# Turning two more normalized slices by DMA instead of the tensor engine, with a new instruction order (two-layer long-convolution and MLP kernel)

## The chip, the core and the metric

The kernel runs on one core of a Trainium2 chip. A core has five engines that run their own instruction streams side by side: TensorE (PE, matrix multiplication and transposes, results in PSUM), VectorE (DVE), ScalarE (ACT), GpSimd (POOL) and SyncE (SP, which here issues nearly all DMAs). They meet through semaphores. The metric is the time of one execution on the device in microseconds (us), lower is better.

## The reference

Four residual steps are applied to a sequence of 2048 rows of 512 channels, in bfloat16: A, B, A, B. Step A is a gated long convolution, step B is an MLP with a GELU.

```
def _A_ref(q, k, v, shift_k, ssm_k, ssm_D):
    ...
    kv = k_shift * v
    ...
    y = y + kv * ssm_D[None, None, :]
    return q * y

def _B_ref(x, w1, b1, w2, b2):
    y = _layernorm(x, axis=-1)
    h = _gelu(jnp.einsum("bsd,df->bsf", y, w1) + b1)
    return jnp.einsum("bsf,fd->bsd", h, w2) + b2

x = A_q
x = x + _A_ref(_layernorm(x, axis=-1), A_k, A_v, A_shift_k, A_ssm_k, A_ssm_D)
x = x + _B_ref(_layernorm(x, axis=-1), B_w1, B_b1, B_w2, B_b2)
x = x + _A_ref(_layernorm(x, axis=-1), A_k, A_v, A_shift_k, A_ssm_k, A_ssm_D)
x = x + _B_ref(_layernorm(x, axis=-1), B_w1, B_b1, B_w2, B_b2)
return x
```

The convolution y depends only on k, v and the filters, not on x. So the kernel computes it once, in a front part, and both A steps use it. After that each row of x goes through the four steps on its own.

## The kernel before

**Front part.** The convolution is a transform over the sequence, done as two stages of small matrix products, a product with the transformed filter, and two inverse stages. The stages that later text names are: the short filter on k and its product with v (lines 800 to 850, for two channel groups on TensorE with L832 behind it, for two on VectorE at L656), the first transform stage (L764), the second stage of the filter (L777) and of the data (L870), the products with the filter (L656 with 128x2048 tiles), the first inverse stage (L894, 256 matmuls) and the second inverse stage (L951, 64 matmuls). The channels are cut into two parts of 64 groups of four (`PARTS`), and products and inverse stages run part by part. Every stage leaves its result in PSUM, and an evacuation copies it to SBUF: L661 when ScalarE does it, L662 when VectorE does. Either engine can take one.

**Row part.** The 2048 rows are 16 slices of 128 rows; slice s is `R_X + s * 512`. Two layers (`L` is 0 and 1) of one A and one B step follow. A layer goes through its slices in blocks: 1, 1, 2, 2, 2, 2, 2, 2, 2 slices in layer 0 and four blocks of 4 in layer 1. For a block, with tags q, y, z, m1 and m2:

- q: mean and variance of each slice on VectorE (L983, L985), the inverse root on POOL (L989, L991), normalization on VectorE (L998)
- y: product with y and residual addition (L656 with 128x512 tiles; 128x256 for the first four slices)
- z: the same statistics and normalization again, into a rotating set of eight buffers
- turning: the first MLP product contracts over channels, so the normalized slice z must be turned, channels into partitions. For slices 0 to 3 of layer 0, TensorE does four 128x128 transposes into PSUM (L1045), and ScalarE or VectorE copies the result to the buffer `R_XT` (L661 or L662). For all other slices, SP issues one `dma_start_transpose` from z to `R_XT` (L1037). There are two `R_XT` buffers, taken by turns of the blocks
- m1: 11 chunks of 4 matmuls (L1058), each followed by ScalarE's GELU (L1063) into `R_HT`
- m2: 11 matmuls per slice (L1091) with a residual addition on VectorE (L1095); the last slice is cut into pieces (L1080, L1084). Finished slices of layer 1 go out by DMA (L645).

**Order.** Nothing in the program text fixes the order of the instructions on an engine. Each piece of work is recorded with `P.op`, with what it reads and writes and with a duration in nanoseconds. `Prog.schedule` then runs a planner: engine by engine it takes the piece that can start first by these durations, and among equals the one of highest priority. It also chooses between ScalarE and VectorE for each evacuation. A DMA takes, in the planner, its issue time and then its bytes at 370 per ns and 2300 ns. Large hand-over tables, keyed by tag or by the running number of the piece, bend the plan: `BIAS` and `PB` are added to priorities, `HOLD` gives an earliest start, `PS` and `SHY` handicap VectorE for an evacuation, and `ENG` forces an evacuation to one engine. On the chip only the resulting order counts, with semaphore waits that `Prog.sync` puts in. SP's queue is in order too: a DMA that waits for its source holds the ones behind it.

Of the kernel before, what the change touches and what calls it, by code (L numbers as in the profile page):

```python
# [44 lines left out]
class Prog:  # L45
# [6 lines left out]
    BIAS = {'': -521155, 'fir0': 1051798, 'fir1': 843097, 'fir2': 989049, 'fir3': 987651, 'h1': 1081037, 'h2': -15927, 'ht': 1112634, 'i1_0': 1897872, 'i1_64':  # L52
        1957624, 'i2_0': 1184460, 'i2_64': 1481308, 'm1': 2555275, 'm2': -1895730, 'q0': 888240, 'q1': 774644, 'q19': 368770, 'q2': 596884, 'q20':
        169092, 'q21': -27345, 'q22': 917115, 'q3': 746810, 'q4': 810080, 'q5': 973212, 'q6': 1402410, 'q7': 321282, 'q8': 747916, 'taps': 871203,
        'warm0': 1001221367, 'x1_0': 904949, 'x1_1': 332081, 'x1_2': 669567, 'x1_3': 179302, 'x2_0': 377722, 'x2_64': 1746588, 'y0': 402006, 'y1':
        377011, 'y19': 351016, 'y2': 526293, 'y20': 1353266, 'y21': 1084298, 'y22': 962110, 'y3': 501697, 'y4': 829124, 'y5': 1453849, 'y6': 1171227,
        'y7': 417695, 'y8': 201523, 'z0': 1335006, 'z1': 1302874, 'z19': 54792, 'z2': 645169, 'z20': 1225188, 'z21': 742421, 'z22': -322863, 'z3':
        -681085, 'z4': 290073, 'z5': -723046, 'z6': 31881, 'z7': 125204, 'z8': 150269}
    SHY = {'fir0': 1381, 'fir1': 0, 'h1': 616, 'h2': 0, 'ht': 1476, 'i1_0': 1122, 'i1_64': 0, 'i2_0': 355, 'i2_64': 600, 'x1_0': 0, 'x1_1': 0, 'x1_2': 0,
        'x1_3': 0, 'x2_0': 175, 'x2_64': 0, 'z0': 1278, 'z1': 0, 'z2': 218}  # L60
    PB = {0: 34576, 2: -79378, 3: 43127, 4: 998812279, 9: 1394230, 44: 1395437, 45: 1613596, 47: 734111, 49: 928776, 51: 998512784, 52: 998468674, 53: -251398,
        54: -275617, 55: -73100, 56: -94401, 57: -104470, 58: -97344, 59: -11254, 60: -108406, 61: -94351, 63: -1000973, 64: -999971, 65: 27771, 66:
        -77522, 67: -999603, 68: 141227, 69: -1000923, 70: -1052691, 71: 34934, 72: -77472, 73: 998216537, 74: 133836, 75: -847532, 76: -193783, 77:
        998086816, 78: 213997, 79: -845232, 80: -158480, 81: 998714645, 82: -29228, 83: 998096074, 85: -912875, 86: 81387, 87: -823698, 88: -168262,
        89: 998118247, 90: 94211, 91: 998328931, 92: 27535, 93: -765996, 94: -165174, 95: -789736, 96: -295, 97: -846123, 99: -845182, 100: -158430,
        101: 998114703, 102: -218608, 103: 998118297, 104: -163885, 105: 998086766, 106: 912895, 107: -54439, 108: 950031, 109: -33246, 110: 1149468,
        111: -31803, 112: 1348311, 113: 217100, 114: 974687, 115: 999587069, 116: 918924, 117: 999198541, 118: 903029, 119: 999587119, 120: 909361,
        121: 217391, 122: 694743, 123: 999618935, 124: 958333, 125: 999612320, 126: 1042905, 127: 219847, 128: 900863, 129: 999657213, 130: 964412,
        131: 999608609, 132: 768388, 133: 999620187, 134: 856071, 135: 999410698, 136: 724031, 137: 999546617, 155: 23799, 156: -162015, 157: -60642,
        158: -461494, 159: -153347, 161: -694106, 162: 1454, 163: -947997, 164: 207759, 165: 998395730, 166: -173754, 167: 998555574, 169: 998332526,  # L70
        170: -423295, 171: 998606664, 172: 38904, 173: 998455595, 175: 999072054, 176: 243913, 177: 154045, 178: 391385, 179: 999289091, 180: 348447,
        181: 999128447, 183: 29584, 184: -999103, 185: 998165866, 186: 998199123, 187: 998019345, 188: 998017691, 189: 998151553, 191: -646236, 192:
        -539651, 193: 998734714, 194: -523620, 195: 998581986, 196: -137633, 197: 998715658, 199: 86734, 200: 998494190, 201: 21973, 202: -495859,
        203: 47162, 204: 48952, 205: 59976, 207: 999452991, 208: -1197, 209: 878201, 210: 929976, 211: 999077641, 212: 730704, 213: 999240348, 215:
        999293389, 216: 725624, 217: 510366, 218: 999271422, 219: 646616, 220: 381726, 221: 999070258, 222: 94055, 223: 349589, 224: 999293339, 225:
        71120, 226: -10853, 227: 772848, 228: 711543, 229: 2558, 230: 999128706, 231: 107444, 232: -203830, 233: 1276613, 234: 384777, 235: -85060,
        236: 790445, 237: 75982, 239: -823960, 240: -697909, 241: 997632090, 242: -339336, 243: -1075953, 244: -656610, 245: -826734, 246: 50, 247:
        -1076003, 248: -339386, 249: 997632040, 250: -210520, 251: -489040, 252: -675432, 253: -825900, 255: -927034, 256: -854615, 257: -1353528,
        258: 997762488, 259: -607871, 260: -1334318, 261: -871126, 262: 997876284, 263: -1321, 264: -704597, 265: 997906582, 266: 148883, 267:
        -675809, 268: -909457, 269: -70780, 270: -56569, 271: -864218, 272: -104560, 273: -36737, 274: -577323, 275: -1480713, 276: -833598, 277:  # L80
        997878740, 279: -1162936, 280: 27, 281: -687297, 282: -121406, 283: -1363624, 284: -118911, 285: 997939634, 286: 577508, 287: -393821, 288:
        475975, 289: -885280, 290: -270112, 291: 997939684, 292: 576726, 293: 998145513, 308: 1177488, 309: 1198831, 310: 1304423, 311: 1244639, 312:
        971190, 314: 285666, 315: -57020, 316: 391644, 317: -46141, 318: 998762253, 319: -155518, 320: 135422, 321: -64658, 322: 346129, 324:
        998409091, 325: -1207668, 326: 998414402, 327: -319349, 328: -1037091, 329: -441577, 330: -1032463, 331: -1024485, 332: -884533, 334: -54361,
        335: -51188, 336: -3436, 337: 322745, 339: -19921, 340: 770364, 341: 119508, 343: 150496, 344: -815052, 345: -1074024, 346: -1087676, 347:
        -942418, 348: -900262, 349: -695458, 350: 351759, 351: -892088, 352: 1076614, 353: -2671, 354: 885814, 355: -1190402, 356: 1001895, 357:
        -1433063, 358: 1027075, 359: -1429074, 360: 1029921, 361: -1731382, 362: 919746, 363: -910238, 364: 41149, 365: -890772, 366: 1184682, 367:
        -897821, 368: -1245948, 369: -144705, 370: -1245720, 371: -401600, 372: 2730439, 373: 4887400, 374: 3740474, 375: 2124032, 377: 112340, 378:
        10032, 379: -338853, 380: -245578, 382: 104508, 383: 805647, 384: -77071, 386: -911065, 387: -70724, 388: -451068, 389: -405580, 390: -950972,
        391: -206569, 392: 187780, 393: 885471, 394: -1662575, 395: 1009734, 396: -1295021, 397: 1024703, 398: -1183431, 399: 1037432, 400: -1248538,  # L90
        401: -255605, 402: -654317, 403: -359159, 405: -1278286, 407: 1092663, 408: -888363, 409: 917474, 410: 814, 411: 890156, 412: -211373, 413:
        -358377, 414: 32750, 415: 5020518, 416: 4338250, 417: 3211311, 418: 2415420, 420: -46159, 421: -2327, 422: -267214, 423: 164122, 424: 265989,
        425: -113051, 427: 110610, 428: 892080, 429: 111401, 430: -44629, 431: -261436, 432: -173254, 433: -363932, 434: 23598, 436: 42311, 437:
        12952, 438: -285134, 439: -300486, 440: 216702, 441: 228190, 442: 255444, 443: 205358, 444: 625548, 445: -22042, 446: 108479, 447: 664113,
        448: 1243693, 449: 863420, 450: -179909, 451: -322256, 452: -471129, 453: 1004937, 454: -629654, 455: 863470, 456: -761928, 457: 1009668, 458:
        -890636, 459: -156707, 460: -292462, 461: -1267645, 462: -913360, 463: -782357, 464: -540612, 465: -252368, 466: -913588, 467: -1302020, 468:
        -435191, 469: -251282, 470: -907822, 471: 3209413, 472: 3720996, 473: 4860599, 474: 3269555, 475: 3378084, 476: 4978144, 477: 4979058, 478:
        2905911, 480: -367979, 481: -368512, 482: -100350, 483: -498935, 484: 138365, 485: -92505, 487: -76592, 488: -174921, 489: 24557, 490: 185584,
# [478 lines left out]
def bass_interleave_layers__ssm_conv_h3__mixer_channel_mlp__prompt_kernel(  # L577
# [348 lines left out]
    for p0, n, o, c in ((0, 128, 0, 10), (0, 96, 10, 1)):  # L926
        d, s = M(p0, n, M_B1 + o, [1, c]), A(p0, n, R_B1 + o, [1, c])
# [204 lines left out]
```

## Time and profile before

| What | us |
|---|---|
| median of 4 runs | 243.22 |
| lowest and highest run | 241.5, 244.19 |
| the profiled execution, its own time | 243.8 |
| its span, first to last instruction | 242.0 |
| POOL busy in it | 34.0 |
| TensorE weight loads, beside the matmuls | 154.0 |
| granted TensorE clock, mean over the span | 1.000 |

The profiled execution took 1.8 us more than its span, and 0.58 us more than the median. In the profile a matmul's row shows start and duration of a pipelined instruction, so the durations of a run of matmuls overlap; from start to start, one of L1091 (512 columns) takes about 0.216 us and one of L1058 with 256 columns about 0.108 us. "x4" behind a row is a count of instructions, and a bracket such as "[0.45 <-POOL sm L991]" says how long the engine was idle just before and what ended it. Instruction names keep their order on one engine, but from one engine to another they have to be matched by time.

### The profile page before, as it was taken

The page shows a single profiled execution, that of the slowest core. Times are in us where ns is not written, and L with a number is a line of the kernel's source. Part 1 is how long each engine was busy: PE and PEld are TensorE (multiplying, and loading weights), DVE is VectorE, ACT ScalarE, POOL GpSimd, SP SyncE. Part 2 cuts the span into 40 slices and gives each one's busy share as a digit, 9 for nine tenths or more (in the row PEclk, how much of TensorE's full clock was granted, in tenths as well). Part 3 has the DMA queues.
Part 4 walks back from the last instruction along what each step waited for, and adds up shares of the span by engine and source line. Part 5 has one row for each costly group of instructions (what it writes and reads, how often), then busy time and mean ns, then how long its engine had stood idle before and what let it go on. Part 6 is the DMA issues. An engine that isn't in the chain of part 4 may idle for free.

```text
span 242.0 us, 5585 instructions
## 1 busy us (share of the span) xinstructions
PE 230.5 (95%) x2338; PEld 154.0 (64%) x2338; DVE 179.4 (74%) x366; ACT 140.1 (58%) x222; POOL 34.0 (14%) x75
## 2 busy tenths in 40 slices
PE   5999999976899999999999999999999999999996
PEld 1887777775889887675775684654444444444444
DVE  0489999999999999889999999999977300202223
ACT  2189999989995996544572471446412774124400
POOL 3250000000104121331232104030111000000000
DMA  6999979999990000211221102407041100411003
GB/s 230 340 384 385 385 163 206 191 195 237 397 362 27 3 0 3 43 23 27 43 43 24 22 1 46 81 7 88 1 87 43 46 0 0 87 43 46 35 30 108
DMA packets 35947, 27.14 MB, mean 112 GB/s; under 512 B 18418, under 2 KB 28881, under 8 KB 35922
## 3 DMA queue, kind: packets, MB, share of 16 engines
q1 hardware_dynamic: 35358, 26.65, 41.4%
q8 instruction: 18, 0.29, 0.5%
q10 hardware_dynamic: 564, 0.14, 0.4%
q14 instruction: 7, 0.06, 0.1%
HBM read 16.82 MB, written 2.10 MB: 78 GB/s over the span
## 4 chain that ended last, share of the span: by engine, by line
PE 57%; DVE 24%; ACT 6%; issue 6%; POOL 4%; DMA 2%; DVEq 0%; POOLq 0%
PE ps L1091 26%; PE ps L1058 26%; DVE ar L656 13%; ACT ar L661 6%; DVE sm L983 4%; DVE ar L662 3%; PE ps L894 3%; POOL ar L739 2%; DMA ar<-ar 2%; DVE ar L832 1%; DVE ar L998 1%; PE ps L1080 1%; DVE sm L985 1%; POOL sm L991 1%; PE ps L870 1%
## 5 line engine op out<-in xcount | busy, mean ns | idle before, releaser
L1063 ACT ACTIVATE ar<-ps,sm 128x256 bf16<-128x256 f32 (+4 forms) x143 | 68.3, 522 | 75.0 <-PE ps L1058 71.3
L1058 PE MATMUL ps<-ar 128*128 128x256 bf16 (+4 forms) x572 | 83.1, 297 | 0.1
L1091 PE MATMUL ps<-ar 128*128 128x512 bf16 (+1 forms) x341 | 79.9, 379 | 0.0
L661 ACT ACTIVATE ar<-ps 128x1024 bf16<-128x1024 f32 (+2 forms) x78 | 70.8, 1026 | 12.5 <-PE ps L764 5.6
L1058 PEld LDWEIGHTS ps<-ar 128*128 128x128 bf16 (+1 forms) x572 | 53.3, 100 | 29.1 <-DMA ar<-ar 0.6
L656 DVE TENSOR_TENSOR ar<-ar 128x512 bf16<-128x512 bf16 (+3 forms) x108 | 64.4, 628 | 1.2 <-ACT ar L661 0.4
L1091 PEld LDWEIGHTS ps<-ar 128*128 128x128 bf16 (+1 forms) x341 | 33.1, 98 | 35.1 <-ACT ar L1063 0.4
L1095 DVE TENSOR_TENSOR ar<-ar,ps 128x512 bf16<-128x512 bf16 x31 | 20.8, 677 | 43.7 <-PE ps L1091 43.6
L983 DVE BATCH_NORM_STATS2 sm<-ar 128x6 f32<-128x512 bf16 (+1 forms) x68 | 42.7, 650 | 0.3
L998 DVE TENSOR_SCALAR ar<-ar,sm 128x512 bf16<-128x512 bf16 x64 | 23.5, 403 | 3.6 <-POOL sm L991 3.6
L991 POOL TENSOR_TENSOR sm<-sm 128x2 f32<-128x2 f32 (+2 forms) x26 | 20.2, 777 | 2.2
L764 PE MATMUL ps<-ar 128*64 128x128 bf16 x512 | 18.0, 222 | 1.4 <-ACT ar L661 0.6
L662 DVE CAST ar<-ps 128x1024 bf16<-128x1024 f32 x16 | 18.9, 1208 | 0.0
L989 POOL TENSOR_SCALAR sm<-sm 128x2 f32<-128x2 f32 (+2 forms) x26 | 5.4, 207 | 91.5 <-DVE sm L985 91.3
L764 PEld LDWEIGHTS ps<-ar 128*64 128x64 bf16 x512 | 15.2, 111 | 4.0 <-ACT ar L661 1.8
L894 PE MATMUL ps<-ar 128*128 128x128 bf16 x256 | 14.8, 219 | 0.9 <-DVE ar L656 0.9
L894 PEld LDWEIGHTS ps<-ar 128*128 128x128 bf16 x256 | 14.4, 113 | 1.2 <-DVE ar L656 1.2
L662 DVE COPY ar<-ps 128x2048 bf16<-128x2048 bf16 (+1 forms) x8 | 7.4, 919 | 10.0 <-PE ps L747 10.0
L870 PE MATMUL ps<-ar 128*128 128x64 bf16 x256 | 9.6, 193 | 3.3 <-ACT ar L661 1.9
L985 DVE BATCH_NORM_AGGREGATE sm<-sm 128x2 f32<-128x6 f32 (+1 forms) x64 | 11.1, 177 | 0.7
L870 PEld LDWEIGHTS ps<-ar 128*128 128x128 bf16 x256 | 8.2, 98 | 4.7 <-ACT ar L661 3.0
L777 PE MATMUL ps<-ar 128*128 128x128 bf16 x128 | 8.7, 220 | 0.5 <-ACT ar L661 0.2
(33 smaller groups left out, 78.0 us busy)
## 6 DMA issues: line engine op xcount, KB each, us to landing
ar<-tab_s SPq DMA_DIRECT2D x16, 256.0 KB, 10.0
ar<-ar SPq DMA_DIRECT2D x16, 256.0 KB, 6.1
ar<-in_A_ssm_k_dram SPq DMA_DIRECT2D x4, 512.0 KB, 6.0
ar<-in_A_k_dram SPq DMA_DIRECT2D x8, 256.0 KB, 7.8
ar<-in_A_v_dram SPq DMA_DIRECT2D x8, 256.0 KB, 9.8
ar<-in_A_q_dram SPq DMA_DIRECT2D x4, 512.0 KB, 8.3
out_dram<-ar SPq DMA_DIRECT2D x7, 256.0 KB, 2.0
ar<-in_B_w_dram SPq DMA_DIRECT2D x1, 1376.0 KB, 12.2
```

The lines of the kernel that those rows point to most:

```text
L656: return P.op(eng, lambda e: e.tensor_tensor(o, a, b, op), dur, reads=[a, b] + list(more), writes=[o])
L661: return e.activation(dst, src(), AF.Copy)
L662: return e.tensor_copy(dst, src())
L764: r = e.matmul(Q(tl, 64 * ri, 64, i * 128, [1, 128]), w, m, start=True, stop=True)
L894: r = e.matmul(Q(tl, 0, 128, i * 128, [1, 128]), w, m, start=q == 0, stop=q == 1)
L983: P.op(DVE, lambda e, sj=sj, x=x: e.bn_stats(sj, x), 40.0 + 1.1 * w, reads=[x], writes=[sj], gate=gate)
L991: P.op(POOL, lambda e: e.tensor_tensor(r, v, hf, ALU.pow), 430.0 + 150.0 * n, reads=[v, hf], writes=[r])
L998: P.op(DVE, lambda e: e.tensor_scalar(o, x, m, r, ALU.subtract, ALU.mult), 335.0, reads=[x, m, r], writes=[o])
L1058: r = e.matmul(Q(tl, 0, rows, 0, [1, w]), a, m, start=dk == 0, stop=dk == 3)
L1063: P.op(ACT, lambda e, dst=dst, tl=tl, rows=rows, bias=bias, w=w: e.activation(dst, Q(tl, 0, rows, 0, [1, w]), AF.Gelu_apprx_tanh, bias=bia ...
L1091: r = e.matmul(Q(tl, 0, 128, 0, [1, 512]), ins[fc][0], ins[fc][1], start=fc == 0, stop=fc == 10)
L1095: P.op(DVE, lambda e, x=x, tl=tl: e.tensor_tensor(x, x, Q(tl, 0, 128, 0, [1, 512]), ALU.add), 640.0, reads=[x], writes=[x], tile=tl)
```

## The change

One condition is changed. In layer 0, slices 2 and 3 now take the branch that slices from 4 on took before: one `dma_start_transpose` each, in place of four TensorE transposes and one evacuation. Slices 0 and 1 keep the tensor engine. Two pieces of work fewer are recorded, so every later running number shifts, and all six tables of the planner are replaced by others; no entry of `PB` or `HOLD` keeps its value. `ENG` forces 46 evacuations in place of 63. Durations, blocks, buffers and the planner itself stay as they are.

```
-    BIAS = {'': -521155, 'fir0': 1051798, 'fir1': 843097, 'fir2': 989049, 'fir3': 987651, 'h1': 1081037, 'h2': -15927, 'ht': 1112634, 'i1_0': 1897872, 'i1_64':
...
-    SHY = {'fir0': 1381, 'fir1': 0, 'h1': 616, 'h2': 0, 'ht': 1476, 'i1_0': 1122, 'i1_64': 0, 'i2_0': 355, 'i2_64': 600, 'x1_0': 0, 'x1_1': 0, 'x1_2': 0,
-        'x1_3': 0, 'x2_0': 175, 'x2_64': 0, 'z0': 1278, 'z1': 0, 'z2': 218}
...
+    SHY = {'fir0': 187, 'fir1': 1275, 'h1': 149, 'h2': 0, 'ht': 1293, 'i1_0': 240, 'i1_64': 0, 'i2_0': 872, 'i2_64': 661, 'x1_0': 794, 'x1_1': 0, 'x1_2': 551,
+        'x1_3': 32, 'x2_0': 0, 'x2_64': 0, 'z0': 1489, 'z1': 1251}
...
+    PS = {83: 479, 87: 603, 89: 792, 95: 971, 99: 0, 101: 0, 107: 63, 163: 1004, 165: 0, 167: 1448, 245: 13, 247: 615, 249: 524, 324: 0, 332: 477}
...
@@ -1032,7 +1029,7 @@
                 z = ntmp()
                 norm(s, mr[i], A(0, 128, z, [1, 512]))
                 dst = A(0, 128, R_XT + k * 2048 + i * 128, [512, 4], [1, 128])
-                if L or s >= 4:
+                if L or s >= 2:
                     zs = A(0, 128, z, [1, 512])
                     P.op(SP, lambda e, zs=zs, dst=dst: e.dma_start_transpose(dst, zs), 1300.0, reads=[zs], writes=[dst],
                          dma=True, nbytes=1 << 17)
```

## The prediction

> **What bounds the kernel now.** I read the page's busy times first, then busy time by stretches, then the rows of the turned slices on each engine, and the chain of waits last. The stretches are cut where the chain changes its engine. Columns: stretch, its length, busy us and count of PE, weight loads, DVE, ACT and POOL, granted clock, DMA share, GB/s.
>
> ```profile
> PE 230.5 (95%) x2338; PEld 154.0 (64%) x2338; DVE 179.4 (74%) x366; ACT 140.1 (58%) x222; POOL 34.0 (14%) x75
> ```
>
> ```profile
> 16.50:71.35 54.85, 48.54 (x1005) 40.84 (x1001) 54.16 (x50) 53.55 (x58) 1.42 (x4) 1.00 1.06 282
> 71.35:85.07 13.72, 13.72 (x188) 12.99 (x189) 13.22 (x34) 10.99 (x14) 3.76 (x10) 1.00 0.13 42
> 85.07:112.60 27.53, 27.40 (x251) 19.82 (x248) 25.28 (x69) 17.53 (x47) 6.14 (x15) 1.00 0.12 21
> 112.60:239.70 127.10, 127.10 (x718) 69.91 (x718) 80.00 (x207) 52.43 (x100) 15.68 (x29) 1.00 0.19 41
> ```
>
> The shares of the whole hide two kernels. From 16.5 to 71.35 DVE and ACT are both full (idle 0.69 and 1.30 us), and PE waits for them. From 71.35 on PE has no hole except one before 112.6: the inverse stages, then m1 and m2 back to back. So after 71.35 only PE work removed, or the hole, can shorten the end. The PE rows of the turned slices (start, duration, line):
>
> ```profile
> 85.07 0.39 PE L1045 MATMUL ps<-ar 128*128 128x128 bf16 x4
> 85.30 0.60 PE L951 MATMUL ps<-ar 128*128 128x256 bf16 x4
> ...
> 91.84 0.39 PE L1045 MATMUL ps<-ar 128*128 128x128 bf16 x4
> 92.06 0.39 PE L1058 MATMUL ps<-ar 128*128 128x128 bf16 x4
> ...
> 93.37 0.39 PE L1045 MATMUL ps<-ar 128*128 128x128 bf16 x4
> 93.60 0.39 PE L1058 MATMUL ps<-ar 128*128 128x128 bf16 x4
> 93.82 0.81 PE L1091 MATMUL ps<-ar 128*128 128x512 bf16 x3
> 94.47 4.32 PE L1058 MATMUL ps<-ar 128*128 128x256 bf16 x40
> ```
>
> The groups at 91.84 and 93.37 are slices 2 and 3; each holds PE 0.22 to 0.23 us until the next start. Their normalizations and evacuations, from DVE's rows and then ACT's:
>
> ```profile
> 90.31 0.38 DVE L998 TENSOR_SCALAR ar<-ar,sm 128x512 bf16<-128x512 bf16 x1
> ...
> 90.70 1.19 DVE L662 CAST ar<-ps 128x1024 bf16<-128x1024 f32 x1
> 91.89 1.06 DVE L998 TENSOR_SCALAR ar<-ar,sm 128x512 bf16<-128x512 bf16 x3
> ...
> 93.87 0.41 DVE L662 COPY ar<-ps 128x512 bf16<-128x512 bf16 x1
> ```
>
> ```profile
> 92.75 0.59 ACT L661 ACTIVATE ar<-ps 128x512 bf16<-128x512 bf16 x1
> ```
>
> z of slice 2 is ready at 90.69, of slice 3 at about 92.27 (first of three, 0.38 each). Turned, they are there at 93.3 and 94.3, and m1 of this block starts at about 94.7, four short matmuls into the row at 94.47. Last, the DMA that the later slices use, and the one place where the chain of waits crosses it:
>
> ```profile
> L1037 SPq DMA_TRANSPOSE ar<-ar x28: 1189/1264/1467, 98.5 to 208.9; - x28
> ...
> DMA to landing us min/median/max: 2.4/2.5/4.7
> ```
>
> ```profile
> 107.49 0.35 DVE ar L998
> 107.84 4.71 DMA ar<-ar
> 112.60 1.49 PE ps L1058 x12
> ```
>
> Issue occupies SP for 1.26 us, landing takes 2.5 us from the issue. The 4.71 us before 112.6 is one of the three slow ones of 28 (3.2, 4.7 and one of 4.6). Between 106 and 113 us the DMA rows show three packets on an instruction queue and one on another, beside the two slow transposes; in other stretches with transposes at 2.5 us there are none or one.
>
> **The change part by part.** The sum is made against the profiled execution's own 243.8 us (span 242.0 and 1.8 around it), 0.58 above the median.
>
> Removed on PE: two groups of four transposes, 2 x 0.225 = 0.45 us, in a stretch where PE is the bound. This is a gain, if the data is not late.
>
> Removed beside it: one evacuation of 0.59 us on ACT and one of 0.41 on DVE. ACT has 10 us idle between 85 and 112.6, so its part is worth nothing. DVE has 2.25 us idle there and produces every z that PE needs next; with 0.33 to 0.41 us less to do, slices 6 and 7 can be ready earlier by as much. That is about the hole before 112.6: the last three L1091 before it start at 111.65 and hold PE until 111.65 + 3 x 0.216 = 112.30, so the hole is 0.30 us. I count it as gone; if the slow landing comes back it stays. Cover for costing ACT at nothing: its GELUs wait 71 us in total for L1058. If it were full there, the gain would be 0.59 more.
>
> Added: two DMA transposes, 2 x 1.26 us on SP. SP has issued nothing since the weights at 59.7 and has slice 4 at 98.5 behind them, so the queue costs nothing; issues at 90.7 and 92.3 end at 93.6. Each waits for its L998, and by the `R_XT` turns for the last m1 matmul of slice 0 (about 89.4). Behind a blocked one stand slice 3's and then slice 4's; PE waits for both before m1 of the block, since each chunk reads both slices. Between end of L998 and issue the trace has 0.03 us (98.50 to 98.53). So slice 2 lands at 93.2 and slice 3 at 92.27 + 0.03 + 2.5 = 94.8, against 94.7 when PE wanted it: 0.1 us late. What is late next is m1 of this block, and PE's cover is m2 of slices 0 and 1: before 94.47 it had issued 15 of their 22 matmuls, so 7 x 0.216 = 1.5 us can be put in front. Stall: zero at 2.5 us, and 94.27 + 2.73 = 97.0, or 2.3 - 1.5 = 0.8 us, if it lands like the slow one. I take zero, since 25 of 28 land so; a new order can also put the 1.19 us CAST at 90.70 behind slice 3's normalization.
>
> A rule that speaks against this step stands beside those rows: the Trainium skill, "VectorE: DVE Perf Modes", section "The three transpose paths", gives a 128x128 bf16 transpose 390 ns on TensorE and 1309 ns by DMA, and its section "Rules for kernel authors" says to use TensorE where a PSUM destination is acceptable. The row first: one L1037 turns four such blocks, 128x512, and lands in 2.5 us. Taken per block, the rule gives 4 x 1.309 = 5.2 us (an estimate): slice 3 would land at 97.5, 2.8 late, 1.3 us of stall after the cover, and the change would lose 1.3 - 0.75 = 0.55. By the row it loses nothing. I take the row. The rule compares latencies; here PE pays 0.225 us of its bound for its shorter one.
>
> The new order: its cost is not in any row, so I bound it. Upwards in speed: in the front, DVE and ACT together have 1.99 us idle between 16.5 and 71.35, so perfect sharing is worth about 1.0. PE is idle 54.85 - 48.54 = 6.3 us there, while all 64 matmuls of L951 (6.7 us) run after 78.5. Half belong to the first channel part; moved into PE's idle time they would free up to 3.4, but then the chain from evacuation to first z (80.27 to 85.07 on DVE and POOL) binds, so I allow 2. Together at most 3. Downwards: every 1024-column evacuation put on the wrong one of two full engines costs DVE 1.21 or ACT 1.06 us, and I see no reason that excludes two or three. In the row part an order that runs out of m2 costs PE directly. Value taken: zero, nearest to the rows, as both orders fill the same full engines. Of the 1024-column evacuations in the front, the new table forces fewer either way, so it does not tell the direction.
>
> Sum: -0.45 (PE) - 0.30 (hole) + 0 (queue, landing) + 0 (order) = -0.75, so 243.05 for an execution like the profiled one, and 242.5 on the scale of the median.
>
> **The rivals.**
>
> *A faster front.* If L951's first half slides into PE's idle time, or DVE and ACT are shared better, m1 starts 2 to 3 us earlier: 239.5 to 240.5. For it: 6.3 us of PE idle in front of a PE-bound rest. Against: the products on DVE that gate L894 run unbroken to 71.2, and L894 (7.2 us) and half of L951 must come after them.
>
> *A slower front, the one on the other side.* Place: DVE and ACT between 16.5 and 71.35. Price: with three evacuations more on DVE than it can carry, 3 x 1.21 = 3.6 us, and everything after 71.35 moves: 242.5 + 3.6 = 246.1. It decides from a net shift of about three on, as two give 244.9, still within 1%. For it: both engines are 97 to 99% busy, so nothing absorbs an error. Against: ACT's idle 1.30 absorbs one.
>
> *Late slices.* Slice 3 lands in 4.7 us and the order has no m2 left to cover: 2.3 us of hole, less the 0.45, and the old hole kept: 243.22 - 0.45 + 2.3 = 245.1. For it: the hole at 112.6 shows exactly this. Against: 25 of 28.
>
> *The turning does nothing.* The removed 0.45 is eaten by other holes and the time stays at 243.2. This can't be told from the forecast.
>
> **How the numbers follow.** One per cent, 2.4 us, is about what a measurement of this kernel can tell from no change. My forecast with small gains or losses of order has 0.41 together with the last rival and most of late slices: its own range is 240.8 to 245.6. Faster front: 0.26. Slower front, with late slices beyond 1%: 0.33, above the faster one because a loss has no floor and the gain has. To hold 8 in 10 the range goes from 239.5, the whole of the allowed gain, to 247.8, which is four evacuations (4.8) and a little stall over 242.5. So: faster 0.26, same 0.41, slower 0.33, time 242.5.
>
> **What would show it.** Right: two groups of L1045 instead of four, 30 of L1037, the first two landing in about 2.5 us near 90 to 95; PE without a hole above 0.3 us after the first m1; the distance from first m1 to the end shorter by 0.4 to 0.8. Wrong: a PE idle row in front of L1058 ended by a DMA near 95, which is late slices; L894's last run beginning 1 us or more away from 71.35, or L951 split by it, which is the front; holes of PE after 100 ended by L998 or L1063, an order that starves. The forecast is wrong if the start of L1058 moves by more than 1.6 us either way.

## The result and the profile after

The changed kernel took 241.91 us (median of 44 runs, 241.29 to 243.71); the kernel before, run beside it, 242.51 (63 runs, 241.5 to 244.96). The ratio is 0.997, 95% interval 0.9957 to 0.9982: 0.6 us faster, a small gain; the interval excludes no change, though the single runs of the two kernels overlap. The profiled execution of the changed kernel took 242.15 us with a span of 240.4, at a granted TensorE clock of 1.000. Line numbers are three lower in the new listing: transposes are L1042, the turning DMA L1034, m1 L1055, m2 L1088, GELU L1060, the inverse stages L891 and L948, normalization L995.

First the page's busy times, then busy time by the same stretches as before (stretch, length, busy us and count of PE, weight loads, DVE, ACT and POOL, clock, DMA share, GB/s).

```profile
PE 229.0 (95%) x2330; PEld 153.1 (64%) x2330; DVE 176.2 (73%) x364; ACT 142.3 (59%) x222; POOL 34.7 (14%) x75
```

```profile
16.50:71.35 54.85, 48.02 (x997) 41.08 (x992) 54.58 (x51) 52.84 (x57) 1.42 (x4) 1.00 1.07 283
71.35:85.07 13.72, 13.72 (x184) 12.54 (x182) 13.31 (x39) 11.80 (x14) 4.06 (x10) 1.00 0.09 29
85.07:112.60 27.53, 27.41 (x245) 20.03 (x243) 23.64 (x69) 17.71 (x49) 7.24 (x16) 1.00 0.17 33
112.60:239.70 127.10, 125.47 (x704) 68.38 (x702) 77.60 (x201) 51.43 (x97) 14.82 (x26) 1.00 0.18 42
```

PE has 8 matmuls fewer, the transposes. In the first stretch DVE is as full as before (54.58 of 54.85); in the others PE is, and the last one falls short of its length only because PE now ends at 238.09, inside it. The shape has not changed: a front bound by DVE and ACT, then PE with one short hole. PE's rows, from the last run of the first inverse stage to m1 of slices 2 and 3:

```profile
70.06 7.34 PE L891 MATMUL ps<-ar 128*128 128x128 bf16 x128 [0.32 <-DVE ar L653]
77.30 6.29 PE L948 MATMUL ps<-ar 128*128 128x256 bf16 x56
83.48 0.40 PE L1042 MATMUL ps<-ar 128*128 128x128 bf16 x4
...
85.37 0.39 PE L1042 MATMUL ps<-ar 128*128 128x128 bf16 x4
85.59 2.01 PE L1055 MATMUL ps<-ar 128*128 128x128 bf16 x28
87.44 1.03 PE L1088 MATMUL ps<-ar 128*128 128x512 bf16 x4
...
92.49 0.39 PE L1055 MATMUL ps<-ar 128*128 128x128 bf16 x4
92.71 2.33 PE L1088 MATMUL ps<-ar 128*128 128x512 bf16 x10
94.88 4.53 PE L1055 MATMUL ps<-ar 128*128 128x256 bf16 x40
```

The hole lies among the 28 m1 matmuls from 85.59 on. At 0.056 us each they would end at 87.15; L1088 behind them starts at 87.44, 0.29 us later. One chunk waits for a GELU (L1060), as the waits of PE's weight loads between 84 and 92 us say (total, times, longest):

```profile
PEld ps L1055 <- ACT ar L1060: 0.3, 1, 0.3
```

DVE's row that makes z of slices 3 and 2, and the two turning DMAs (the answer for that line between 85 and 93 us):

```profile
88.69 0.70 DVE L995 TENSOR_SCALAR ar<-ar,sm 128x512 bf16<-128x512 bf16 x2
```

```profile
L1034 SPq DMA_TRANSPOSE ar<-ar x2: 1188/1252/1317, 89.1 to 90.5; - x2
...
DMA to landing us min/median/max: 2.5/2.5/2.5
```

Both slices are normalized by 89.4, the DMAs go out at 89.1 and 90.5 and land 2.5 us later, the second at 93.0. Ten m2 matmuls stand in front of m1 of slices 2 and 3, which begins at 94.88: the data is there 1.9 us before it is wanted, and the row of L1055 has no bracket. So the turning costs no wait.

Where the time went is not read from the two profiled executions alone. L891's last run starts at 70.06 where L894's started at 71.35, 1.3 us earlier. PE ends where the chain of waits turns to DVE, before and after:

```profile
239.72 0.02 issue
```

```profile
238.09 0.02 issue
```

From L891 to there it is 238.09 - 70.06 = 168.03 us, and was 239.72 - 71.35 = 168.37: 0.34 less. The eight transposes (0.45) and the hole of 0.30 in front of 112.6, which is not there any more, make 0.75; the new hole takes 0.29 back, and 0.12 is not accounted for. The 1.3 us in the front belongs to that one execution of the kernel before; the experiments come back to it.

### The profile page after: what moved, and what is told of

The parts are those of the page before. It is cut to its first block, busy times and chain, and to the rows that moved or that the text cites. A ratio compares the mean times of both kernels' runs of the same rounds, so it can differ in the third digit from the quotient of the medians.

```text
span 240.4 us, 5575 instructions
## 1 busy us (share of the span) xinstructions
PE 229.0 (95%) x2330; PEld 153.1 (64%) x2330; DVE 176.2 (73%) x364; ACT 142.3 (59%) x222; POOL 34.7 (14%) x75
## 4 chain that ended last, share of the span: by engine, by line
PE 75%; DVE 10%; ACT 6%; DMA 4%; issue 2%; SPq 1%; POOL 0%; ACTq 0%; DVEq 0%; POOLq 0%
PE ps L1055 31%; PE ps L1088 31%; DVE ar L653 6%; ACT ar L658 6%; PE ps L891 3%; DMA ar<-ar 3%; PE ps L761 3%; DVE ar L659 2%; PE ps L822 2%; PE ps L744 2%; DMA ar<-in_A_shift_k_dram 1%; PE ps L1077 1%; SPq L642 1%; DVE sm L980 1%; PE ps L805 1%
## 5 line engine op out<-in xcount | busy, mean ns | idle before, releaser
L1060 ACT ACTIVATE ar<-ps,sm 128x256 bf16<-128x256 f32 (+4 forms) x143 | 68.2, 522 | 72.3 <-PE ps L1055 69.1
L1055 PE MATMUL ps<-ar 128*128 128x256 bf16 (+5 forms) x572 | 84.7, 297 | 0.1
L1088 PE MATMUL ps<-ar 128*128 128x512 bf16 (+1 forms) x341 | 81.7, 379 | 0.0
L658 ACT ACTIVATE ar<-ps 128x1024 bf16<-128x1024 f32 (+2 forms) x78 | 73.1, 1043 | 9.8 <-PE ps L744 2.5
L1055 PEld LDWEIGHTS ps<-ar 128*128 128x128 bf16 (+1 forms) x572 | 53.4, 100 | 30.0 <-ACT ar L1060 1.6
L653 DVE TENSOR_TENSOR ar<-ar 128x512 bf16<-128x512 bf16 (+3 forms) x108 | 63.4, 627 | 0.4
L1088 PEld LDWEIGHTS ps<-ar 128*128 128x128 bf16 (+1 forms) x341 | 33.1, 98 | 34.1 <-ACT ar L1060 0.5
L995 DVE TENSOR_SCALAR ar<-ar,sm 128x512 bf16<-128x512 bf16 x64 | 23.7, 404 | 6.8 <-POOL sm L988 6.6
L659 DVE CAST ar<-ps 128x1024 bf16<-128x1024 f32 (+1 forms) x16 | 18.6, 1178 | 0.1
L891 PE MATMUL ps<-ar 128*128 128x128 bf16 x256 | 14.8, 219 | 0.9 <-DVE ar L653 0.9
L891 PEld LDWEIGHTS ps<-ar 128*128 128x128 bf16 x256 | 14.4, 113 | 1.1 <-DVE ar L653 1.1
L659 DVE COPY ar<-ps 128x2048 bf16<-128x2048 bf16 (+1 forms) x6 | 5.7, 954 | 9.3 <-PE ps L744 9.3
```

Of the source, the lines that this page charges most:

```text
L653: return P.op(eng, lambda e: e.tensor_tensor(o, a, b, op), dur, reads=[a, b] + list(more), writes=[o])
L658: return e.activation(dst, src(), AF.Copy)
L659: return e.tensor_copy(dst, src())
L891: r = e.matmul(Q(tl, 0, 128, i * 128, [1, 128]), w, m, start=q == 0, stop=q == 1)
L995: P.op(DVE, lambda e: e.tensor_scalar(o, x, m, r, ALU.subtract, ALU.mult), 335.0, reads=[x, m, r], writes=[o])
L1055: r = e.matmul(Q(tl, 0, rows, 0, [1, w]), a, m, start=dk == 0, stop=dk == 3)
```

## Experiments

The new order and the removed transposes came together, so the first runs take them apart. To run one without the other, the planner is replaced by the lists of pieces that it had put out, one list for each engine; numbers in the diffs are running numbers of pieces. The tables being gone, line numbers are smaller: m1 is L920 or L921, m2 L953 or L954, the transposes L907 to L909, the normalization L860 or L861, the second stage of the data L732 or L733. A kernel "in the old order" has the lists of before, "in the new order" those of after.

**The edit alone, old order, nothing else moved.** 447 and 444 are the transposes of slices 3 and 2; later numbers shift.

```
-                if L or s >= 4:
+                if L or s >= 2:
...
- 'tensor': ... 403, 447, 407, 373, 405, 444, 411, 374, 453, 449 ...
+ 'tensor': ... 403, 407, 373, 405, 411, 374, 451, 447 ...
```

> The edit alone in the old order: slices 2 and 3 turned by DMA, their eight transposes and two evacuations taken out, every other instruction at its old place. Theory 'the edit' (the gain is 0.45 us of TensorE and the hole before 112.6): in this order nothing is put in front of the block's m1. z of slice 2 is ready at 92.94 (it is the third of the three L998 at 91.89, not the first), lands at 95.5, and TensorE is there 0.45 earlier than before, at 94.25, so a hole of about 1.2 us opens there and the kernel is 0.3 to 0.8 us slower than before, ratio 1.001 to 1.003. Theory 'the order' (the edit is worth nothing, the new order brought the gain): the landing is hidden or not, the time stays at 1.000 or above. This run shows the hole or not; the next one tells the theories apart.

Measured: 245.84 us (6 runs) against 242.59 (51 runs), ratio 1.0144, interval 1.0098 to 1.0191. The same edit that makes the changed kernel faster makes this one 3.25 us slower. PE's rows, then the chain of waits (start, length, what):

```profile
91.81 0.81 PE L953 MATMUL ps<-ar 128*128 128x512 bf16 x3
95.30 1.92 PE L920 MATMUL ps<-ar 128*128 128x256 bf16 x16 [2.68 <-DMA ar<-ar]
```

```profile
90.21 1.05 DVE ar L860 x3
91.26 0.03 DVE ar L518
91.29 3.96 DMA ar<-ar
95.25 0.05 issue
95.30 2.81 PE ps L920 x24
```

The hole is larger than expected, and two things set it. The chain names the z that is late: it comes out of the third of three normalizations. Slice 3 is normalized earlier in this order, and slice 2 is that third one. Landing in 2.5 us, it would have been there at 93.8, 1.3 us after the last m2 matmul. But its DMA took 3.96 us, 1.5 more. Between 93 and 94 us the DMA queues held one packet of instruction code beside the transpose (packets, MB, share of the engines):

```profile
q1 hardware_dynamic: 134, 0.03, 13.9%
q8 instruction: 1, 0.02, 5.5%
```

The hole of about 2.8 us (95.30 - 91.81 - 3 x 0.216) less the transposes' 0.45 explains 2.4 of the 3.25 us.

**The same, with cover.** The last 7 m2 matmuls of slice 1 (416, 417), one m1 chunk of slice 1 (401) and three GELUs are moved in front of m1 of slices 2 and 3.

```
- 'tensor': ... 407, 373, 405, 411, 374, 451, ... 453, 401, ... 461, 416, 417, 473 ...
+ 'tensor': ... 407, 373, 401, 405, 411, 374, 416, 417, 451, ... 453, ... 461, 473 ...
- 'scalar': ... 371, 414, 452, 406, 448, 412, 460, 454, 402, 450 ...
+ 'scalar': ... 371, 414, 402, 406, 412, 452, 448, 460, 454, 450 ...
```

> The same, with the remaining seven m2 matmuls of slice 1 (and the one m1 chunk and three GELUs that they need) moved in front of m1 of slices 2 and 3: 1.5 us of cover. Theory 'the edit': no hole near 95, 0.45 to 0.75 us faster than before, ratio 0.997 to 0.998. Theory 'the order': 1.000 within its interval. If the seven matmuls are missed later, a hole of some 0.2 us before m1 of slices 4 and 5 near 102.

Measured: 242.97 us (22 runs), ratio 1.0009, interval 0.9979 to 1.0039.

```profile
92.22 2.33 PE L953 MATMUL ps<-ar 128*128 128x512 bf16 x10
94.39 2.78 PE L920 MATMUL ps<-ar 128*128 128x256 bf16 x24
```

The hole is gone, and with it 2.9 us. So the missing cover is what made the edit alone slow. But a gain of 0.45 is not seen either. The interval of 0.3% to each side would not show it, and 10 of the 22 runs have a lowered TensorE clock, which comes up below; the other 12 have a median of 242.44, against 242.11 for the kernel before at full clock, so they don't show a gain either.

**The transposes back, new order.** Slices 2 and 3 go through the tensor engine again; their transposes are 447 and 444, put in after 401 and after 403, with an evacuation on ACT and one on DVE.

```
-                if L or s >= 2:
+                if L or s >= 4:
...
- 'tensor': ... 401, 413, 373, 403, 374 ...
+ 'tensor': ... 401, 447, 413, 373, 403, 444, 374 ...
```

> The new order with the edit undone: slices 2 and 3 turned by TensorE again, one evacuation on ScalarE and one on VectorE, put in where the engines come by after the normalization, all else at its new place. Theory 'the edit': the gain goes, 0.45 to 0.75 us slower than the changed kernel, ratio to before 1.000 (0.9985 to 1.0015). Theory 'the order': the gain stays, ratio 0.997. Either way L891 starts its last run at the same time as in the changed kernel.

Measured: 242.24 us (14 runs), ratio 0.9982, interval 0.9954 to 1.0009. By medians the order alone is worth 0.35 of the gain and the transposes 0.33 (242.24 to 241.91); each by itself is within what this run can tell from nothing, and the second compares two sets of runs (the kernel before had 242.59 in the one and 242.51 in the other).

**The price of a transpose.** Into the changed kernel each of slices 2 and 3 gets 16 transposes back, beside the DMA, into a PSUM tile that nobody reads: added work only. The changed kernel was run again in the same comparison.

```
+                    for j in range(16 if s0 == 4 else 4):
...
- 'tensor': ... 401, 413, 373, 403, 374 ...
+ 'tensor': ... 401, 448, 413, 373, 403, 445, 374 ...
```

> The changed kernel with 32 transposes on TensorE, 16 for slice 3 and 16 for slice 2, that nobody reads, at two places between 91 and 93; the DMA transposes stay and nothing is evacuated. Four times the eight that the edit removed. Theory 'TensorE bounds the row part': 32 x 0.056 = 1.8 us in full, ratio 0.0074 above the changed kernel (1.0045 to before), so that eight cost 0.45. Rival 'the removed time was idle time anyway' (something else, data or GELU, ends the waits there): clearly less than 1.8, 0 to 0.9 us.

> The changed kernel once more, instruction by instruction, beside the next two: 0.997 again (0.995 to 0.9985), its times in a narrow band (most within 1 us of its fastest), while those of the kernel before reach 2.5 us above theirs.

Measured: 243.79 us (12 runs) with 32 transposes and 241.97 (12 runs) without: 1.82 us, 0.057 us for each, and 8 x 0.057 = 0.45 us for the eight of the change. Against the kernel before, of which 29 runs had a median of 242.94, the repeated changed kernel has a ratio of 0.9958 (0.993 to 0.9985) and the other 1.0025 (0.9996 to 1.0054). The rows of the added work:

```profile
91.49 1.06 PE L909 MATMUL ps<-ar 128*128 128x128 bf16 x16
...
93.69 1.06 PE L909 MATMUL ps<-ar 128*128 128x128 bf16 x16
```

From 91.49 to the next start, 92.39, PE is held for 0.90 us: 0.056 for one. The duration in the row, 1.06, overlaps what follows.

**One slice more by DMA.** Slice 1 is turned by DMA as well, and two m1 chunks of slice 1 are moved behind the first m2 group of slice 0 (372).

```
-                if L or s >= 2:
+                if L or s >= 1:
...
- 'tensor': ... 362, 393, 405, 372, 411 ...
+ 'tensor': ... 362, 372, 392, 404, 410 ...
```

> The changed kernel with slice 1 turned by DMA too, and two m1 chunks of slice 1 moved behind the first four m2 matmuls of slice 0, so that they start near 87.4. z of slice 1 is ready at 84.27 and lands at 86.8. Theory 'the edit': hidden, 0.23 us of TensorE less than the changed kernel, ratio to before about 0.996. Rival 'latency': this early there is no work to cover 2.5 us, TensorE idles 0.5 us or more in front of m1 of slice 1 and the time is the changed kernel's or worse, ratio 0.998 or above.

Measured: 242.08 us (22 runs), ratio 0.998 (0.9961 to 1.0), no better than the changed kernel.

```profile
86.08 0.81 PE L954 MATMUL ps<-ar 128*128 128x512 bf16 x3 [0.28 <-ACT ar L926]
...
87.58 2.07 PE L921 MATMUL ps<-ar 128*128 128x128 bf16 x32 [0.24 <-ACT ar L926]
```

No wait on the DMA, but two for GELUs (L926), 0.52 us together and more than the four transposes give (0.23). A second version also puts one more m1 chunk of slice 0 (364) in front of the first m2 group and one of slice 1 (now 410) later, and moves the GELUs of slice 0 ahead of those of slice 1:

```
- 'scalar': ... 355, 359, 394, 406, 363, 369, 412, 396 ...
+ 'scalar': ... 355, 359, 363, 365, 369, 393, 405, 395 ...
```

> Slice 1 by DMA as in the fourth run, where TensorE then waited 0.28 and 0.24 us for GELUs. Here one more m1 chunk of slice 0 stands in front of the first m2, the GELUs of slice 0 come first on ScalarE, and slice 1 begins with four chunks in a row. If the waits for GELUs had eaten that gain: no PE hole between 84 and 90, 0.2 to 0.3 us faster than the changed kernel, 0.996 to before. If landing is the limit: a hole ended by the DMA before the first chunk of slice 1 near 87.

Measured: 241.86 us (12 runs), ratio 0.9952 (0.9924 to 0.998). One GELU wait of 0.37 us is left, at 89.13. It is 0.11 us under the changed kernel of the same comparison, which these runs can't tell from nothing.

**What spreads the times of the kernel before.** Over all comparisons its 178 runs reach from 241.41 to 245.0 us, with quartiles of 242.07 and 243.33. The 56 runs of the changed kernel reach from 241.29 to 243.71, quartiles 241.74 and 242.11: 37% of the former and 4% of the latter lie over 1.5 us above their lowest. Two things go with the long runs, a lowered clock and a stop of PE.

*The clock.* For 115 of the 178 runs, and for every run of the other kernels, the mean granted TensorE clock is on record:

| | runs | clock of 0.993 or less |
|---|---|---|
| kernel before | 115 | 43 |
| its five variants in the old order | 64 | 28 |
| changed kernel and its variants, new order | 128 | 0 |

The 43 low ones of the kernel before have a median of 243.92 us, the other 72 (0.999 or 1.000) of 242.26. Over 242.91, which is 1.5 above the lowest, lie 38 of the 43 and 5 of the 72. Four of the profiled executions are low ones. In each the loss is in one stretch of 3.4 us at half the clock. Here is the stretch in the run with cover (the clock is the third number from the end), with PE's row that follows the idle time before it (L670, the short filter on k):

```profile
18.00:21.50 3.50, 3.50 (x74) 3.50 (x70) 3.50 (x4) 2.16 (x3) 0.00 (x0) 0.51 1.06 389
```

```profile
16.71 1.14 PE L670 MATMUL ps<-ar 128*128 128x128 bf16 x16 [2.02 <-DMA ar<-in_A_k_dram]
```

The same two rows of the evacuation run, which comes below:

```profile
54.00:57.50 3.50, 3.44 (x64) 3.02 (x60) 2.36 (x2) 2.92 (x4) 0.00 (x0) 0.52 1.16 223
```

```profile
53.41 2.07 PE L733 MATMUL ps<-ar 128*128 128x64 bf16 x46 [2.33 <-issue]
```

Three of the four come at about 18 us, after PE has waited 2.02 to 2.32 us for k; the fourth comes after a stop of 2.33 us. Idle time alone does not decide it: one of 2.61 us, in the warm-up run below, is not followed by a low clock. In the seven profiles of the new order PE waits 0.59 us for k at most, and none of its idle times between 8 and 30 us is longer than 1.20 us. That the new order keeps its clock for this reason is argued and not shown: no run changed that wait alone.

*The stop.* The profiled execution of before was a long one (243.8) at full clock, and the trace shows a place where it lost time, in the second stage (L870):

```profile
47.50 2.04 PE L764 MATMUL ps<-ar 128*64 128x128 bf16 x62 [0.22 <-issue]
49.47 2.45 PE L870 MATMUL ps<-ar 128*128 128x64 bf16 x66
53.16 1.52 PE L870 MATMUL ps<-ar 128*128 128x64 bf16 x46 [1.24 <-issue]
```

PE stops in the middle of a group of equal matmuls, and no semaphore releases it ("issue"). Two theories of it were tried, a slow start of TensorE (more warm-up matmuls ahead) and an evacuation that holds up the next stage (the second evacuation of the filter's transposition moved from DVE to ACT).

```
-    warm(dconv, 6, 512, 213.5)
+    warm(dconv, 9, 512, 213.5)
```

> The kernel before with nine instead of six warm-up matmuls (L711) at the very start; all else is the same. Theory 'slow start': the old order's executions differ because TensorE's matmuls run at half rate until somewhere between 5 and 12 us, and in the late ones VectorE reaches the k taps (L656) after k has landed at 16.6, up to 1.1 us late. Longer warm-up leaves no idle time between warm-up and the first transposes, the rate doubles sooner, VectorE waits for k at 16.6 in most executions, and the upper quarter of the times falls: ratio 0.997 to 0.9985, close to the changed kernel. Theory 'the edit' alone: how the start goes does not matter for the difference, ratio 1.000 (up to 0.3 us slower, if the taps at L730 come later).

Measured: 243.21 us (12 runs), ratio 1.0038 (1.0006 to 1.0069).

```profile
48.71 2.37 PE L733 MATMUL ps<-ar 128*128 128x64 bf16 x63
53.69 1.60 PE L733 MATMUL ps<-ar 128*128 128x64 bf16 x49 [2.61 <-issue]
```

```
- 'scalar': [0, 1, 3, 2, 4, 51, 52, 79 ...
+ 'scalar': [0, 1, 3, 2, 4, 51, 52, 66, 79 ...
```

> The kernel before with one part of the new order's front alone: the evacuation of the second filter transpose (128x2048) goes to ScalarE, which is idle there, as in the changed kernel; VectorE is 1.2 us ahead before k lands. Theory 'slow start': the late executions lose nothing any more, upper quarter down, ratio 0.997 to 0.999; the fastest executions stay where they are (241.4). Theory 'the edit' alone: 1.000.

Measured: 242.64 us (12 runs), ratio 1.0007 (0.9981 to 1.0033).

> The previous one with the edit and the moved cover (seven m2 matmuls and what they need in front of m1 of slices 2 and 3). With the start out of the way, theory 'the edit' gives 0.45 us less than the previous kernel, ratio to before 0.995 to 0.997. Theory 'the edit is worth nothing': the previous kernel's ratio. Theory 'landing': transposes issued at 91.3 run into an instruction fetch near 93 in part of the executions, land 1 to 2 us late, and the cover of 1.5 us does not always do: wide spread, ratio 0.998 to 1.001.

That one is the last move together with the edit and its cover, in the old order. Measured: 242.9 us (12 runs), ratio 1.0024 (0.9996 to 1.0051).

> The changed kernel with nine warm-up matmuls. Theory 'slow start': the new order has the evacuation on ScalarE and loses at most 0.5 us to a late start, so there is little left to gain: 0 to 0.3 us faster than the changed kernel, ratio to before 0.996 to 0.997. If warm-up delays the first transposes: 0.998.

That one is the warm-up in the new order. Measured: 241.88 us (12 runs), ratio 0.9975 (0.9947 to 1.0004).

```profile
48.98 2.34 PE L733 MATMUL ps<-ar 128*128 128x64 bf16 x62
52.61 1.15 PE L733 MATMUL ps<-ar 128*128 128x64 bf16 x34 [1.29 <-issue]
```

Both theories fell: no time was gained. But the rows told what the stop is. In before it comes after 66 matmuls of its group; with three warm-up matmuls more, after 63. In the new order the run with 32 extra transposes (which come later) stops after 65, the one with three warm-up matmuls more after 62. So it is tied to the count of instructions and not to the data. From the "issue" row before it to the stop there are 62 + 66 = 128 matmuls, each with a weight load: 256 instructions. The page's queue line of before shows the code arriving in packets of 0.29 MB / 18 = 16 KB:

```profile
q8 instruction: 18, 0.29, 0.5%
```

PE had to wait for code: in before the packet lands at 51.63 us (50.24 + 1.39) and PE goes on at 53.16, 1.53 us later. In all six profiles with a stop this distance is 1.47 to 1.64 us, while the stops differ by more than a factor of two. The other queue's transfers kept the DMA engines full from 44 to 54 us; that they delay the code was not tried. The Trainium skill, "Runtime: NRT & Kernel Launch", section "Instruction fetch mechanics", says that code comes in blocks of 256 instructions through a DMA queue of the engine's own, at a cost "mostly hidden". The packets agree; the cost, 1.06 to 2.61 us where a stop occurs, does not.

Stops appear in the profiles of before, of the warm-up run, of the evacuation run and of the one with edit and cover (1.24, 2.61, 2.33 and 1.51 us), which is 4 of 6 in the old order, and in 2 of 7 in the new one (1.29 and 1.06). Why fewer in the new order is not shown. The stretch before it has longer short waits there (0.28 and 0.29 us in the run with extra transposes, 0.23 and 0.19 in the warm-up run), which give the code more time to arrive; no run changed that alone.

What each costs can be read from the start of the last run of the first inverse stage. In the old order it is 69.67 and 69.85 us in the two profiles without a stop, and 71.08 to 72.25 in the four with one. In the new order it is 69.22 to 70.06 in the five without, 70.15 and 70.91 in the two with one. So a stop moves everything behind it. Half the clock at 18 us does not by itself: the run with cover had it, no stop, 69.85 and a time of 241.72. Three of the four profiled executions with the low clock have a stop too; why low clock and long run go together so often in the other runs stays open, as their stops are not on record.

## Why the prediction was right, and where its sum was not

A gain of 0.75 was forecast; measured are 0.6 us (242.51 to 241.91) and, in the repetition, 0.97 (242.94 to 241.97). Both lie within 1%, the case that had the largest chance. The size depends on how many runs of the kernel before have the low clock: 12 of 29 in the repetition, and its other 17 have a median of 242.27, only 0.30 above the changed kernel. The absolute 242.5 came out 0.6 too high because it was put on the median of four runs, 243.22; over 63 runs the kernel before has 242.51.

- *The transposes, -0.45.* Right. The run with 32 extra ones gives 0.057 us each, so 0.45. Putting the eight back in the new order cost 0.33, a little less, within what these runs can tell.
- *The queue and the landing, +0.* Right in the changed kernel: 2.5 us for both, and data 1.9 us early. The estimate from the Trainium skill's block price ("VectorE: DVE Perf Modes", "The three transpose paths") would have put the second landing at 90.5 + 5.2 = 95.7, 0.8 us after m1's start, where no wait is; the row was the right one to take.
- *When z is ready.* The prediction took slice 2's z from the row at 90.31 and slice 3's from the first of the three at 91.89. This step failed: 90.31 is slice 3's, and slice 2's is the third of the three, ready at 91.89 + 1.06 = 92.95, 0.7 us later than the latest that it reckoned with. In the changed kernel this does not show because the new order has both done by 89.4. In the old order, with no cover moved and a slow landing, the late-slice rival came true: 245.84, where it had said 245.1.
- *The cover.* Right, and needed: 7 m2 matmuls, 1.5 us, put in front. The changed kernel does just that (10 of L1088 in front of L1055), and the old order with the same move loses its hole.
- *The hole before 112.6, -0.30.* Mis-sized: worth about zero. In the profiles of the warm-up run and of the evacuation run, both in the old order with the tensor engine's transposes, PE has no wait on a DMA after 80 us. The hole was seen in one of three profiled executions with those transposes in the old order, so it can't be counted on as a gain. It is gone in the changed kernel's profile, but the new order has one of 0.29 of its own, for a GELU, ahead of the first m2 at 87.44.
- *The order, +0.* Mis-sized: worth about -0.35 by medians (242.59 to 242.24). The two errors cancel in the sum, which is luck. It is not the faster-front rival: at the lower quartile the new order with the old transposes (242.08) equals the kernel before (242.07), and only from there up does it win, 242.52 against 243.33 at the upper quartile. The transposes, in turn, show at the lower quartile (241.74, 0.34 less). The clock tells the two kinds of run apart: in that comparison the 30 runs of the kernel before at full clock have a median of 242.11, no slower than 242.24, and the 21 at low clock have 244.27. All 14 runs in the new order are at full clock. So what the order brings is that the long, low-clock runs are gone; whether the clock or the stop makes them long is not shown. The prediction spoke of neither, though the bracket "issue" stood in the profile.
- *The profile to compare with.* In the execution profiled before, L894's last run began 1.3 us later than in the one after, about the length of its stop, 1.24. So the two profiled executions differ by 243.8 - 242.15 = 1.65 where the medians differ by 0.6. By this, one of the prediction's signs of being wrong came true, the start of L894 more than 1 us away. It was meant for a faster front; but old-order executions without the stop start it at 69.67 and 69.85, so the one before was late.

## What to carry to other kernels

Before a transpose is handed from the tensor engine to a DMA, work out when its source is ready, add the landing, and put as much other tensor work in front of the reader; here the same edit lost 3.25 us without that work and gained 0.33 to 0.45 in the new order, which has it. Where a row says x3, find out which of the three is the one that is waited for, by its order on the engine that comes next. And look at the spread of the runs, and at the granted clock of each, before comparing two profiles: a long execution brings holes that a typical one does not have, and an order of instructions can gain by having fewer such runs.

## What the hardware showed unexpectedly

- TensorE can stall for its own instructions: 1.06 to 2.61 us, at a fixed count of instructions, and it goes on 1.47 to 1.64 us after the packet of code has landed. The DMA engines were full meanwhile.
- The granted TensorE clock fell to half for 3.4 us in 4 of 13 profiled executions, each time after 2.0 to 2.3 us without work (a pause of 2.61 us had no such effect), and runs of one kernel differ in it: 43 of 115 of the kernel before, none of 128 in the new order.
- A DMA transpose of 128x512 lands in 2.5 us, but in 3.96 where a packet of instruction code was on a DMA queue beside it; the slowest in the changed kernel took 4.4. That the packet is the cause was not tried by itself.
- Transposes in a stream occupy TensorE for 0.056 us each, as a 128-column matmul of L894 does (128 of them in the 7.17 us from 71.35 to 78.52), although four of them read as 0.39 us in the rows.
